# A tuned attention-and-two-MLPs kernel: a fourth raw weight buffer, two q/k buffers, a shorter warm-up, and a new order

## The chip, the cores and the metric

The kernel runs on one core of a Trainium2 chip. The metric is the device time of one execution in microseconds. The kernel before took 869.03 us (median of three runs, 868.75 to 869.29).

## What is computed

Attention over 4 sequences of 576 tokens with 8 heads of 64, causal within a window of 128 and with a linear distance bias; then two MLPs on the 2304 x 512 result, 512 to 2048 and back. The first has a rational activation, the second x * sigmoid(x).

```python
mask = (rel >= 0) & (rel < 128)                     # rel = query - key
attn = softmax(where(mask, q @ k.T / 8 - slope[h] * rel, -1e9))
x = (attn @ v).reshape(2304, 512)
h = x @ w_in;  P = a0 + a1*h + a2*h**2 + a3*h**3
x = (P / (1 + |b0|*|h| + |b1|*h**2 + 1e-6)) @ w_out
h = x @ w2_in;  out = (h / (1 + exp(-h))) @ w2_out
```

The MLP weights arrive as 64-bit floats, so a raw tile of 128 x 512 weights is 512 KB.

## The kernel before

**Arithmetic.** Each MLP operand is split in two rounded parts, high and low (`xh` and `xl`, `gh` and `gl`, two halves of a weight tile), and each product is three matmuls: high x high, high x low, low x high. The second MLP uses a seven-product scheme for 2 x 2 blocks (`CHAIN`), so its weights are first combined into seven "forms", which are written to memory (`prep`) and streamed back (`stream_in`).

**Stages.** The 18 token tiles are cut into blocks of 4, 4, 3, 4 and 3 tiles. For a block, attention runs in four groups (a pair of heads each): scores on PE (L698), a predicated copy for the masked part (L704) and the masked maximum (L711) on DVE, the exponential on ACT (L715), the row sums' reciprocal on DVE (L726, L727), the normalisation on POOL (L734), transposes on PE (L754), two mask products (L799 and L803 on DVE, or L785 and L786 on POOL), and the product with v on PE (L831). Its result is cut into `xh` on ACT and `xl` on DVE (L855) or, for some groups of block 0, with a further copy on ACT and the subtraction on POOL (L851; option `xl00` to `xl03`). Then come the block's 16 steps of the first MLP (L889 to L891 for `h`, L958 to L960 for `acc`), among which the attention of a later block is mixed. The second MLP runs in three token groups, each with a phase A (`z_a`) and a phase B (`z_b`).

**First-MLP weights.** For each of 16 steps a raw tile of the first weights (`w1`) and one of the second (`wo1`) is loaded by SP (L549), made into fp32 by two steps on ACT (L561, L564) and one on DVE (L567), and split: high part by ACT or POOL (L474), low part by a subtraction on POOL (L485). That subtraction is the last reader of the raw tile. All raw tiles share the tag `wraw` with three buffers (`stb`).

**Order.** No engine chooses its work while the kernel runs: `Plan` is a list scheduler that, while the program is built, places each operation on an engine with assumed costs, assumed DMA landing times (`LAG` is added to what depends on a load) and a priority (lower first; about one unit per step of the first MLP). The order in which it places the operations is the order of each engine's instructions, and an engine waits for the head of its queue. The numbers in `OPT` are engine choices and offsets of priorities: `pw` and `pwo` for the first MLP's weights, `qlead` and `vlead` for the loads of q/k and v, `pw2` and `pwo2` for the forms of the second MLP, `tlead`, `hlead`, `xlead`, `slead` for the second MLP. `SHIFTS` adds a number to the priorities of runs of operations.

**Spins.** `first_spin` issues `warm` matmuls on the identity, whose result nobody reads. While the program is emitted, gaps of over 300 planned ns on PE in the first part are filled with more:

```python
if free is not None and o.start - free > OPT["fillmin"] and not first_acc and not (first_h and live):
    pl.spin(int((o.start - free) * OPT["fill"] / c_pe4(P)), ...)     # c_pe4(128) = 215.8, fill = 0.6
```

The planner's times for the start are: identity ready on POOL at 700 + 600, 89 to PE, `warm` x 427, 110 for a stall; the first q/k load issued at 730, landed at 730 + 2000 + 720, then `LAG` 1400 and 100.

**q and k.** Each group loads `kd` and `qd` (L627; L636 for the first group, in two parts) into a ring of `qkb` buffers each.

Of the kernel before, what the change touches and what calls it, by code (L numbers as in the profile page):

```python
# [9 lines left out]
F32 = mybir.dt.float32  # L10
F32R = mybir.dt.float32r
I32 = mybir.dt.int32
# [8 lines left out]
NT, DM, DFF = B * S, H * D, 2048  # L21
P = 128
# [10 lines left out]
OPT = {  # L33
    'blk1': '4,4,3,4,3',
    'res': 0,
    'lag': 2,
    'gh': 'act|pool',
    'gl': 'dve|pool',
    'whi': 'act|pool',
    'wlo': 'pool',  # L40
    'norm': 'pool',
# [4 lines left out]
    'hb': 2,  # L46
    'eb': 2,
    'ptb': 1,
    'qkb': 3,
    'vb': 3,  # L50
    'tabs': 'pool',
    'stb': 3,
    'strb': 3,
    'wpro': 0.256,
    'dS': -1.52,
    'dT': 0.037,
    'dA': 0.149,
    'dm': 0.366,
    'look': 0.451,
    'pw': -0.72,  # L60
    'pwo': -0.374,
    'dg': -5.616,
    'lead': 2.536,
    'slk': 0,
    'warm': 6,
    'fill': 0.6,
    'fillmin': 300.0,
    'fs': 10,
    'ob': 3,
    'pl': -0.721,  # L70
    'vlead': -1.233,
    'qlead': -1.974,
    'keen': 9999.0,
    'norm0': 'pool',
    'sq': 'act',
# [4 lines left out]
    'mk02': 'dd',  # L80
    'mk03': 'dd',
    'xl00': 'd',
    'xl01': 'd',
    'xl02': 'p',
    'xl03': 'd',
    'alt': 0,
    'gh0': 'act|dve',
    'gl0': 'pool',
    'la': 8.921,
    'lb': 302.617,  # L90
    'dm2': 1.231,
    'sums': 'pool',
    'fhi': 'act|pool',
    'flo': 'dve|pool',
# [1 line left out]
    'xsum': 'dve|pool',  # L96
    'xfh': 'act|pool',
    'xfl': 'pool',
    's1': 'act',
    'tsum': 'pool',  # L100
    'th': 'act|dve',
    'tl': 'dve|pool',
    'tlead': 1.016,
    'hlead': -0.505,
    'oq': 'sp',
    'pw2': 511.696,
    'rw2': 25.851,
    'pwo2': 1331.915,
    'rwo2': 14.569,
    'xlead': -0.854,  # L110
    'slead': 0.691,
    'shift': 'act',
    'tail': 1,
}
# [1 line left out]


SHIFTS = [
# [6 lines left out]
]  # L125


# [28 lines left out]
           for b in ("pe", "act", "dve", "pool", "sp")}  # L156
LATENCY["pe", "pe"] = 0
PORT_GAP = 60.0
LAG = {"kd": 1400.0, "qd": 1400.0, "vh": 1400.0, "wraw": 1200.0, "ws": 400.0, "wv": 400.0, "tab": 0.0}
FREE0 = (700.0, 730.0)  # L160
STALL = 110.0

# [9 lines left out]
class Plan:  # L172
# [11 lines left out]
    def op(self, prio, eng, cost, fn, reads=(), writes=(), after=(), dma=False):  # L184

        o = Op()
        o.eng, o.cost, o.fn, o.prio, o.idx = eng, cost, fn, prio, len(self.ops)
        o.alts = eng if isinstance(eng, dict) else {eng: (cost, fn)}

        o.banks = {t[:2] for t in list(reads) + list(writes) if t[0] in ("h", "atA", "atB") or t[0].startswith("acc")}  # L190
        o.port = {e for e in o.alts if e == "pool" or e == "dve" and not o.banks}
        o.deps, o.allocs = set(after), []
        o.dma = dma or eng == "sp"
        o.lag = max([LAG.get(t[0], 0.0) for t in writes], default=0.0) if o.dma else 0.0
        for t in list(reads) + list(writes):
            key, reg = t[:2], t[2:]
            if key not in self.tile_ops:
                self.tile_ops[key] = []
                o.allocs.append(key)
            else:  # L200
                o.deps.add(self.tile_ops[key][0])
            self.tile_ops[key].append(o)
        for t in reads:
            key, reg = t[:2], t[2:]
            for w, r in self.writers.get(key, ()):
                if not reg or not r or r == reg:
                    o.deps.add(w)
        for t in writes:
            key, reg = t[:2], t[2:]
            for w, r in self.writers.get(key, ()):  # L210
                if not reg or not r or r == reg:
                    o.deps.add(w)
            for w, r in self.readers.get(key, ()):
                if not reg or not r or r == reg:
                    o.deps.add(w)
        for t in reads:
            self.readers.setdefault(t[:2], []).append((o, t[2:]))
        for t in writes:
            self.writers.setdefault(t[:2], []).append((o, t[2:]))
        o.deps.discard(o)  # L220
        self.ops.append(o)
        return o
# [166 lines left out]
def plan_kernel(ctx, tc, qn, kn, vp, table, w1, wo1, w2, wo2, out):  # L389
    nc = tc.nc if tc is not None else None  # L390
    BLK1 = [int(x) for x in OPT["blk1"].split(",")]
    NMAX = max(BLK1) * P
    NB1MAX = max(BLK1)
    RES, LAG = OPT["res"], OPT["lag"]
    pl = Plan()
# [12 lines left out]
    act = pool("act", OPT["actb"])  # L408
    gpool = pool("g", OPT["gb"])
    evac = pool("evac", OPT["ob"])  # L410
    stage = pool("stage", OPT["stb"])
# [9 lines left out]
    def apool(name, bufs):  # L421
        return att_stack.enter_context(tc.tile_pool(name=name, bufs=bufs)) if tc is not None else None
# [4 lines left out]
    pt_p = apool("pt", OPT["ptb"])  # L427
    st_p = apool("st", 4)
    tab_p = apool("tabs", 1)
    for t in ("kd", "qd"):  # L430
        pl.tag(t, OPT["qkb"])
    pl.tag("vh", OPT["vb"])
# [81 lines left out]
        T[("h", "spin")] = h_p.tile([P, 512], F32, tag="h", name="spin")  # L514
        spin(OPT["warm"])

    pl.op(-98, "pe", 427 * OPT["warm"], first_spin, reads=[("ident", 0)], writes=[("h", "spin")])
    pl.spin = spin

    late = []  # L520

    def late_consts():
        for part, cols in ((0, slice(0, 3 * P)), (1, slice(3 * P, 6 * P + 16))):
            pl.op(-91.0 + 0.5 * part, "sp", 700, lambda cols=cols: nc.sync.dma_start(tab_all[:, cols], table[:, cols]), writes=[("tab", part)])
        for part in range(2):
            for h in range(H):
                pl.op(-70 + 0.1 * h + 10 * (h // 2) + 25 * part, do_copy("act" if h + part == 0 else OPT["tabs"], 2 * P,
                      lambda h=h, part=part: (tabs[:, h, 2 * part:2 * part + 2], tab[:, 4 * part:4 * part + 2]), scale=-8.0 * 2.0 ** -(h + 1)), 0, None,
                      reads=[("tab", part)], writes=[("tabs", h, part)])
        late.append(("na", 0))  # L530
        late.append(("ab", 0))
        pl.op(-3, "dve", 80, lambda: nc.vector.tensor_scalar(out=na, in0=coef[:, 0:4], scalar1=-1.0, scalar2=None, op0=ALU.mult),
              reads=[("tab", 1)], writes=[("na", 0)])
        pl.op(-3, "act", 200, lambda: nc.scalar.activation(out=ab, in_=coef[:, 4:6], func=AF.Abs), reads=[("tab", 1)], writes=[("ab", 0)])
# [6 lines left out]
        return r[:, :, 1].bitcast(F32) if wide else r  # L541

    def raw_weight(name, f, src, p, load_p):
        rk = ("wraw", f"{name}{f}")

        def load():
            if wide:
                raw = stage.tile([P, DM, 2], I32, tag="wraw", name=f"raw_{name}{f}")
                nc.sync.dma_start(raw, src.bitcast(I32).rearrange("p (c two) -> p c two", two=2))  # L549
            else:  # L550
                raw = stage.tile([P, DM], F32, tag="wraw", name=f"raw_{name}{f}")
                nc.sync.dma_start(raw, src)
            T[rk] = raw

        pl.op(load_p, "sp", 1500 if wide else 728, load, writes=[rk])
        if wide:


            top = lambda: T[rk][:, :, 1].bitcast(F32)
            low = lambda: T[rk][:, :, 0].bitcast(U32)  # L560
            pl.op(p - 0.6, "act", c_act(NR) + 45, lambda: nc.scalar.activation(out=top(), in_=top(), func=AF.Prelu, scale=2.0 ** -112, alpha=2.0 ** 32),  # L561
                  reads=[rk + (1,)], writes=[rk + (1,)])
            pl.op(p - 0.5, any_of(OPT["shift"], {
                "act": (c_act(NR) + 45, lambda: nc.scalar.activation(out=low(), in_=low(), func=AF.Copy, scale=LOW_SCALE)),  # L564
                "dve": (c_dve2x(NR), lambda: nc.vector.tensor_scalar(
                    out=low(), in0=low(), scalar1=29, scalar2=None, op0=ALU.logical_shift_right))}), 0, None, reads=[rk + (0,)], writes=[rk + (0,)])
            pl.op(p - 0.3, "dve", c_dve(NR), lambda: nc.vector.scalar_tensor_tensor(  # L567
                out=top().bitcast(U32), in0=top().bitcast(U32), scalar=3, in1=low(), op0=ALU.logical_shift_left, op1=ALU.bitwise_or),
                reads=[rk], writes=[rk + (1,)])
        return rk  # L570
# [421 lines left out]
    lead = OPT["lead"]  # L992
# [65 lines left out]
        pools["v"] = ctx.enter_context(tc.tile_pool(name="stream2", bufs=3))  # L1058
        pools["s"] = ctx.enter_context(tc.tile_pool(name="xsums", bufs=2))

    last_att = [o for k, l in pl.tile_ops.items() if k[0] in ("kd", "qd", "vh", "e", "ph", "m", "l", "tab", "tabs") for o in l]
    opener = pl.op((nb1 - 1) * KF + 1.0, "sp", 0, open2, after=last_att)
    for j in range(NF):
        pl.tag(f"F{j}", 1)
# [395 lines left out]
```

## Time and profile before

| | |
|---|---|
| Median of three runs | 869.03 us |
| Profiled execution | 869.16 us |
| Its span | 867.3 us |
| PE / DVE / ACT / POOL busy | 855.2 / 643.1 / 603.1 / 637.9 us |
| Moved by DMA | 228.94 MB, 264 GB/s on average |

Times in the trace are microseconds from the start of the span. PE is TensorE, DVE VectorE, ACT ScalarE, POOL GpSimd, SP the engine that issues most loads. Matmuls overlap, so the time from one start to the next says more than a matmul's own duration. A wait is named by what it waited for last.

### The profile page before, as it was taken

How to read it: one execution, taken by the hardware profiler on the slowest of the kernel's cores; microseconds unless marked ns; L12 is line 12 of the kernel's file. 1: busy time of each engine (PE TensorE's matmuls, PEld its weight loads, DVE VectorE, ACT ScalarE, POOL GpSimd, SP SyncE). 2: the span in 40 equal slices, each digit the busy share in tenths (PEclk: the TensorE clock that was granted, in tenths of full speed). 3: DMA queues.
4: the chain of work that ended last, by engine and by line, in shares of the span. 5: the costliest groups of instructions: out<-in, count | busy, mean ns of one | idle time of the engine just before them, and what ended most of it. 6: DMA issues, size and time to landing. Idle time of an engine off the chain costs nothing.

```text
span 867.3 us, 15300 instructions
## 1 busy us (share of the span) xinstructions
PE 855.2 (99%) x5076; PEld 765.1 (88%) x5076; DVE 643.1 (74%) x1308; ACT 603.1 (70%) x1291; POOL 637.9 (74%) x613
## 2 busy tenths in 40 slices
PE   8989999999999999999999999999999999999998
PEld 6667778877788998777889999999999999999998
DVE  7899897789999898998889984357733477433652
ACT  6699997799888988887889984446434365344452
POOL 4778845666888897878899677479954599744884
PEclk9999999999999999999999999999999999999999
DMA  7746764586889887876797889898888888878884
GB/s 253 264 161 214 243 223 137 169 277 227 289 310 321 294 280 263 306 255 238 275 349 240 295 297 356 262 318 281 281 277 250 292 288 282 295 248 258 252 269 169
DMA packets 80462, 228.94 MB, mean 264 GB/s; under 512 B 8192, under 2 KB 17152, under 8 KB 80384
## 3 DMA queue, kind: packets, MB, share of 16 engines
q1 hardware_dynamic: 78080, 219.59, 76.2%
q10 hardware_dynamic: 2304, 8.39, 2.4%
q8 instruction: 40, 0.66, 0.3%
q14 instruction: 38, 0.31, 0.1%
HBM read 178.66 MB, written 49.28 MB: 263 GB/s over the span
## 4 chain that ended last, share of the span: by engine, by line
PE 82%; DVE 5%; ACT 4%; POOL 3%; DMA 3%; issue 2%; SPq 0%; ACTq 0%; POOLq 0%; DVEq 0%
PE acc L958 6%; PE h L889 6%; PE acc L960 6%; PE acc L959 6%; PE h L891 5%; PE h L890 5%; PE z_a L1233 4%; PE z_b L1300 4%; PE z_a L1234 4%; PE z_a L1235 4%; PE z_b L1301 4%; PE z_b L1299 4%; PE bank_atA L831 3%; PE bank_atA L698 2%; PE bank_atA L1233 1%
## 5 line engine op out<-in xcount | busy, mean ns | idle before, releaser
L485 POOL TENSOR_TENSOR xl_b<-g,xh_b 128x384 fp32r<-128x384 f32 x81 | 90.6, 1119 | 69.6 <-ACT xh_b L466 67.8
L466 ACT CAST xh_b<-g 128x384 fp32r<-128x384 f32 x162 | 83.0, 514 | 64.3 <-PE z_b L1301 42.0
L958 PE MATMUL acc<-gh,wo 128*128 128x512 f32 (+1 forms) x320 | 121.1, 378 | 0.0
L960 PE MATMUL acc<-gl,wo 128*128 128x512 f32 (+1 forms) x320 | 118.7, 371 | 0.1
L959 PE MATMUL acc<-gh,wo 128*128 128x512 f32 (+1 forms) x320 | 117.8, 368 | 0.0
L481 DVE TENSOR_TENSOR xl_b<-g,xh_b 128x384 fp32r<-128x384 f32 x87 | 87.3, 1014 | 30.3 <-ACT xh_b L466 29.1
L485 POOL TENSOR_TENSOR gl<-t,gh 128x512 fp32r<-128x512 f32 (+1 forms) x76 | 93.0, 1224 | 15.9 <-ACT gh L466 12.5
L385 ACT ACTIVATE g<-t_a 128x384 f32<-128x384 f32 x72 | 37.9, 526 | 75.2 <-DVE t_a L378 75.2
L485 POOL TENSOR_TENSOR g<-g,g 128x384 f32<-128x384 f32 x72 | 84.5, 1185 | 2.0
L889 PE MATMUL h<-xh,ws 128*128 128x512 f32 (+1 forms) x224 | 84.2, 376 | 0.4 <-DVE t L934 0.4
L891 PE MATMUL h<-xh,ws 128*128 128x512 f32 (+1 forms) x224 | 82.2, 367 | 0.0
L890 PE MATMUL h<-xl,ws 128*128 128x512 f32 (+1 forms) x224 | 82.1, 367 | 0.0
L958 PEld LDWEIGHTS acc<-gh,wo 128*128 128x128 f32 x320 | 60.1, 188 | 13.4 <-issue 5.6
L960 PEld LDWEIGHTS acc<-gl,wo 128*128 128x128 f32 x320 | 60.0, 188 | 9.5 <-POOL gl L485 1.5
L959 PEld LDWEIGHTS acc<-gh,wo 128*128 128x128 f32 x320 | 60.1, 188 | 6.7
L1233 PE MATMUL z_a<-xf,w2s 128*128 128x384 f32 x192 | 64.2, 335 | 0.0
L1235 PE MATMUL z_a<-xf,w2s 128*128 128x384 f32 x192 | 64.1, 334 | 0.0
L1234 PE MATMUL z_a<-xf,w2s 128*128 128x384 f32 x192 | 64.1, 334 | 0.0
L1299 PE MATMUL z_b<-xh_b,wo2s 128*128 128x384 f32 x192 | 64.1, 334 | 0.0
L1300 PE MATMUL z_b<-xl_b,wo2s 128*128 128x384 f32 x192 | 64.1, 334 | 0.0
L1301 PE MATMUL z_b<-xh_b,wo2s 128*128 128x384 f32 x192 | 64.1, 334 | 0.0
L715 ACT ACTIVATE e<-e,m 128x128 f32<-128x128 f32 x144 | 56.0, 392 | 7.6 <-DVE m L711 7.3
(207 smaller groups left out, 2701.9 us busy)
## 6 DMA issues: line engine op xcount, KB each, us to landing
w2s<-forms_w SPq DMA_DIRECT2D x84, 512.0 KB, 4.7
wo2s<-forms_wo SPq DMA_DIRECT2D x84, 512.0 KB, 4.6
ws<-sc SPq DMA_DIRECT2D x64, 512.0 KB, 4.4
raw_w<-in_w SPq DMA_DIRECT2D x32, 512.0 KB, 4.9
raw_wo<-in_wo SPq DMA_DIRECT2D x32, 512.0 KB, 4.9
forms_w<-st_w SPq DMA_DIRECT2D x24, 512.0 KB, 5.0
forms_wo<-st_wo SPq DMA_DIRECT2D x24, 512.0 KB, 4.9
sc<-w ACTq DMA_DIRECT2D x16, 512.0 KB, 5.2
```

Of the source, the lines that this page charges most:

```text
L485: nc.gpsimd.tensor_tensor(out=o, in0=a, in1=b, op=op)
L889: nc.tensor.matmul(o, lhsT=T[W][:, 0, c], rhs=xh, start=kt == 0, stop=False)
L890: nc.tensor.matmul(o, lhsT=T[W][:, 0, c], rhs=xl, start=False, stop=False)
L891: nc.tensor.matmul(o, lhsT=T[W][:, 1, c], rhs=xh, start=False, stop=kt == KD - 1)
L958: nc.tensor.matmul(a, lhsT=T[WO][:, 0, c], rhs=T[G1][:, :n], start=first_f, stop=False)
L959: nc.tensor.matmul(a, lhsT=T[WO][:, 1, c], rhs=T[G1][:, :n], start=False, stop=False)
L960: nc.tensor.matmul(a, lhsT=T[WO][:, 0, c], rhs=T[G2][:, :n], start=False, stop=last_f)
L1233: nc.tensor.matmul(o, lhsT=w(0, kt * P), rhs=x[:, 0, kt], start=st and kt == 0, stop=False, skip_group_check=True)
L1234: nc.tensor.matmul(o, lhsT=w(0, kt * P), rhs=x[:, 1, kt], start=False, stop=False, skip_group_check=True)
L1235: nc.tensor.matmul(o, lhsT=w(1, kt * P), rhs=x[:, 0, kt], start=False, stop=kt == 1, skip_group_check=True)
L1299: nc.tensor.matmul(o, lhsT=w(0, m * P), rhs=h, start=st and q == 0, stop=False, skip_group_check=True)
L1300: nc.tensor.matmul(o, lhsT=w(0, m * P), rhs=l, start=False, stop=False, skip_group_check=True)
```

## The change

The raw tiles of the first MLP's odd second weights (`wo1`, f = 1, 3, ...) get a tag and a pool of one buffer of their own; this pool closes with the attention's pools. The rings of `kd` and `qd` have two buffers in place of three. `warm` is 3 in place of 6. In the planner the warm-up and the table loads are assumed longer, and `LAG` is not added for a tile with index 0, which is the first group's `kd`, `qd` and `vh`. Four engine choices change (`xl01`, `gl0`, `s1`, `th`), many priority offsets change, and `SHIFTS` is a new list (only its first entries are shown), so the order on every engine is planned anew.

```diff
-    'qkb': 3,
+    'qkb': 2,
-    'wpro': 0.256,
-    'dS': -1.52,
-    'dT': 0.037,
-    'dA': 0.149,
-    'dm': 0.366,
-    'look': 0.451,
-    'pw': -0.72,
-    'pwo': -0.374,
-    'dg': -5.616,
-    'lead': 2.536,
+    'wpro': 0.249,
+    'dS': -1.551,
+    'dT': -0.036,
+    'dA': 0.112,
+    'dm': 0.165,
+    'look': 2.085,
+    'pw': -0.374,
+    'pwo': 0.042,
+    'dg': -2.108,
+    'lead': 2.551,
-    'warm': 6,
+    'warm': 3,
-    'pl': -0.721,
-    'vlead': -1.233,
-    'qlead': -1.974,
+    'pl': 0.045,
+    'vlead': -2.618,
+    'qlead': -0.035,
-    'xl01': 'd',
+    'xl01': 'p',
-    'gl0': 'pool',
-    'la': 8.921,
-    'lb': 302.617,
-    'dm2': 1.231,
+    'gl0': 'dve|pool',
+    'la': 17.853,
+    'lb': 163.905,
+    'dm2': -0.281,
-    's1': 'act',
+    's1': 'act|dve',
-    'th': 'act|dve',
+    'th': 'act',
-    'tlead': 1.016,
-    'hlead': -0.505,
+    'tlead': 21.962,
+    'hlead': -5.152,
-    'pw2': 511.696,
-    'rw2': 25.851,
-    'pwo2': 1331.915,
-    'rwo2': 14.569,
-    'xlead': -0.854,
-    'slead': 0.691,
+    'pw2': 67.228,
+    'rw2': 2.912,
+    'pwo2': 2440.758,
+    'rwo2': 12.704,
+    'xlead': -33.586,
+    'slead': 1.745,
 SHIFTS = [
-    (47, 4, -0.61), (257, 3, 0.14), (291, 1, 1.63), (341, 4, 0.79), (437, 26, -0.03), (546, 6, 0.48), (734, 76, 0.18), (882, 57, -0.68),
+    (73, 1, 2.51), (181, 1, 0.25), (282, 12, 1.4), (332, 11, 0.63), (497, 25, 0.81), (532, 42, 0.22), (565, 62, 0.01), (644, 63, 0.03),
...
-LAG = {"kd": 1400.0, "qd": 1400.0, "vh": 1400.0, "wraw": 1200.0, "ws": 400.0, "wv": 400.0, "tab": 0.0}
+LAG = {"kd": 1400.0, "qd": 1400.0, "vh": 1400.0, "wraw": 1200.0, "wrawA": 1200.0, "ws": 400.0, "wv": 400.0, "tab": 0.0}
-        o.lag = max([LAG.get(t[0], 0.0) for t in writes], default=0.0) if o.dma else 0.0
+        o.lag = max([LAG.get(t[0], 0.0) for t in writes if t[1] != 0], default=0.0) if o.dma else 0.0
+    raw_p = apool("raw", 1)
+    pl.tag("wrawA", 1)
-    pl.op(-98, "pe", 427 * OPT["warm"], first_spin, reads=[("ident", 0)], writes=[("h", "spin")])
+    pl.op(-98, "pe", 470 * OPT["warm"], first_spin, reads=[("ident", 0)], writes=[("h", "spin")])
-            pl.op(-91.0 + 0.5 * part, "sp", 700, lambda cols=cols: nc.sync.dma_start(tab_all[:, cols], table[:, cols]), writes=[("tab", part)])
+            pl.op(-91.0 + 0.5 * part, "sp", 1150, lambda cols=cols: nc.sync.dma_start(tab_all[:, cols], table[:, cols]), writes=[("tab", part)])
-        rk = ("wraw", f"{name}{f}")
+        own_pool = name == "wo1" and f % 2
+        rk = ("wrawA" if own_pool else "wraw", f"{name}{f}")
-                raw = stage.tile([P, DM, 2], I32, tag="wraw", name=f"raw_{name}{f}")
+                raw = (raw_p if own_pool else stage).tile([P, DM, 2], I32, tag=rk[0], name=f"raw_{name}{f}")
-    last_att = [o for k, l in pl.tile_ops.items() if k[0] in ("kd", "qd", "vh", "e", "ph", "m", "l", "tab", "tabs") for o in l]
+    last_att = [o for k, l in pl.tile_ops.items() if k[0] in ("kd", "qd", "vh", "e", "ph", "m", "l", "tab", "tabs", "wrawA") for o in l]
```

## Rows read from the trace of the kernel before

**Rows 1.** The page's first part: busy us, share of the span, instructions of each engine.
```profile
PE 855.2 (99%) x5076; PEld 765.1 (88%) x5076; DVE 643.1 (74%) x1308; ACT 603.1 (70%) x1291; POOL 637.9 (74%) x613
```

**Rows 2.** Windows: stretch, length, busy us per engine (instructions), granted clock, DMA share, GB/s.
```profile
0.00:60.00 60.00, 52.92 (x471) 38.64 (x471) 50.03 (x191) 44.13 (x145) 39.14 (x52) 1.00 0.70 239
515.00:863.00 348.00, 348.00 (x2008) 347.58 (x2007) 181.66 (x250) 159.04 (x316) 243.23 (x207) 1.00 0.85 275
...
700.00:750.00 50.00, 50.00 (x291) 50.00 (x290) 36.42 (x40) 25.05 (x48) 48.31 (x35) 1.00 0.87 279
...
10.00:12.00 2.00, 1.53 (x28) 1.22 (x30) 1.93 (x17) 2.00 (x13) 1.26 (x4) 1.00 1.05 405
```

**Rows 3.** Waits of PE from 60 us on: total us, times, longest.
```profile
PE h L889 <- DVE t L934: 1.6, 2, 1.2
```

**Rows 4.** PE's spins in 0 to 60 us: xcount, busy us, mean ns, idle before.
```profile
L511 PE MATMUL spin<-ident 128*128 128x128 f32 x62 | 10.6, 322 | 1.4 <-POOL ident masks.py:199 1.4
...
L511 PE MATMUL bank_acc<-ident 128*128 128x128 f32 x38 | 5.4, 283 | 0.0
```

**Rows 5.** Timeline of the start: start us, us, engine line op, tiles, xcount [idle before].
```profile
0.74 0.38 SPq L636 DMA_DIRECT2D kd<-in_kn  x1
1.17 0.42 SPq L636 DMA_DIRECT2D qd<-in_qn  x1
1.36 3.78 PE L511 MATMUL spin<-ident 128*128 128x128 f32 x16 [1.36 <-POOL ident masks.py:199]
4.47 0.42 ACT L466 ACTIVATE tabs<-tab 128x256 f32<-128x256 f32 x1 [2.46 <-DMA tab<-in_table]
5.07 0.57 PE L698 MATMUL bank_atA<-kd,qd 64*128 64x128 f32 x1
6.18 1.16 PE L511 MATMUL spin<-ident 128*128 128x128 f32 x8
6.30 0.29 DVE L704 COPY_PREDICATED bank_atA<-tab,bank_atA 128x128 f32<-128x128 uint32 x1 [2.11 <-PE bank_atB L698]
```

**Rows 6.** DMA issues of 0 to 1.6 us, then 4.9 to 5.9 us: KB, median us to landing.
```profile
kd<-in_kn SPq DMA_DIRECT2D x1, 128.0 KB, 2.2
qd<-in_qn SPq DMA_DIRECT2D x1, 128.0 KB, 2.1
...
qd<-in_qn SPq DMA_DIRECT2D x1, 256.0 KB, 5.3
```

**Rows 7.** Timeline of POOL: bias tables of the second part, first normalisation.
```profile
7.06 4.33 POOL L474 TENSOR_SCALAR tabs<-tab 128x256 f32<-128x256 f32 x10 [0.65 <-DMA tab<-in_table]
...
12.00 2.04 POOL L734 TENSOR_TENSOR e<-e,l 128x512 f32<-128x512 f32 x2 [0.61 <-DVE l L727]
```

**Rows 8.** Timeline around the third group's scores: SP, PE and DVE.
```profile
7.00 1.81 SPq L549 DMA_DIRECT2D raw_w<-in_w  x3
10.85 0.34 PE L698 MATMUL bank_atA<-kd,qd 64*128 64x128 f32 x1 [0.47 <-DMA qd<-in_qn]
...
15.31 0.29 DVE L711 CUSTOM_DVE_ANT_0 e<-bank_atA,tabs 128x128 f32<-128x128 f32 x1 [1.18 <-PE bank_acc L754]
15.53 0.69 DVE L799 TENSOR_TENSOR ph<-bank_acc,tab 128x512 f32<-128x512 f32 x1
...
16.94 0.51 DVE L803 TENSOR_TENSOR ph<-bank_acc,ph 128x384 f32<-128x384 f32 x1
```

**Rows 9.** Timeline and chain of 31 to 42 us: subtractions, raw tile, ACT's wait.
```profile
31.35 0.68 DVE L855 TENSOR_TENSOR xl<-bank_acc,xh 128x512 fp32r<-128x512 f32 x1
32.89 1.31 POOL L485 TENSOR_TENSOR w<-raw_w,w 128x512 fp32r<-128x512 f32 x1
34.23 6.79 DMA raw_w<-in_w
38.63 1.28 POOL L851 TENSOR_TENSOR xl<-xf,xh 128x512 fp32r<-128x512 f32 x1
41.09 0.69 ACT L561 ACTIVATE raw_w<-raw_w 128x512 f32<-128x512 f32 x1 [3.35 <-DMA raw_w<-in_w]
```

More of the change, by code (lines that the diff above doesn't have):

```diff
@@ L543, in raw_weight @@
     def raw_weight(name, f, src, p, load_p):
-        rk = ("wraw", f"{name}{f}")
+        own_pool = name == "wo1" and f % 2
+        rk = ("wrawA" if own_pool else "wraw", f"{name}{f}")
         def load():
             if wide:
-                raw = stage.tile([P, DM, 2], I32, tag="wraw", name=f"raw_{name}{f}")
+                raw = (raw_p if own_pool else stage).tile([P, DM, 2], I32, tag=rk[0], name=f"raw_{name}{f}")
                 nc.sync.dma_start(raw, src.bitcast(I32).rearrange("p (c two) -> p c two", two=2))
             else:
-                raw = stage.tile([P, DM], F32, tag="wraw", name=f"raw_{name}{f}")
+                raw = (raw_p if own_pool else stage).tile([P, DM], F32, tag=rk[0], name=f"raw_{name}{f}")
                 nc.sync.dma_start(raw, src)
```

10 rows, old and new, of the table SHIFTS are left out of this document.

## Prediction

> **What bounds the kernel now.** The page comes first: TensorE is busy 99% of the span and no other compute engine above 74% [rows 1]. A busy PE need not be doing useful work, so the windows come next: from 515 to 863 us PE is busy 348.00 of 348 us [rows 2], and the waits from 60 us to the end come to 1.6 us in two waits, the longer 1.2 us [rows 3]. After 60 us an order can therefore give back at most 1.6 us, and can lose without limit. The first 60 us are different: 10.6 + 5.4 = 16.0 us of PE's "busy" time there are spins (L511: matmuls on the identity whose result nobody reads), and PE is idle for another 60 - 52.92 = 7.1 us [rows 2, 4]. Attention of block 0 runs there through PE, DVE (50.03 of 60 us), ACT (44.13) and POOL (39.14) [rows 2]: no engine is full, the chain between them is the bound. So the change is priced in the first 60 us, and what starts earlier there reaches the end only if the 800 us behind it stay as dense.
>
> **Shorter warm-up and the planner's landing time.** The first real matmul starts at 5.07 us, behind 16 spin instructions that last from 1.36 to 5.14 [rows 5]. An fp32 matmul shows as two instructions, so these are 8: six asked for, two fillers. The count comes from the code. Before: the spins end for the planner at 1389 + 6 x 427 + 110 = 4061 ns, the first scores at 3450 + 1400 + 100 = 4950, and int(889 x 0.6 / 215.8) = 2. After: 1389 + 3 x 470 + 110 = 2909; the lag of 1400 no longer counts for group 0, so 3550; int(641 x 0.6 / 215.8) = 1. That is 4 matmuls, 8 instructions, half of 3.78 us: over at about 1.36 + 1.9 = 3.3 us. The data are there by then: k is issued at 0.74 and lands 2.2 us later, q at 1.17 and 2.1 us later, so 2.9 and 3.3 us [rows 5, 6]. First scores at about 3.4 us in place of 5.07: 1.65 us earlier. What is late next? The DVE mask (L704), at 6.30 now, needs 1.15 us of scores and the first table, for which ACT waited until 4.47: 4.6 us, so DVE keeps the 1.65. POOL doesn't: it scales ten of the bias tables from 7.06 on, when the second table has landed, until 7.06 + 4.33 = 11.39 us, and the first normalisation (L734), which stands on the chain, starts at 12.00 [rows 5, 7]. On that branch only 0.61 us can be kept. The ends are 0.6 and 1.65; I take the middle, -1.1, since the chain leaves POOL for DVE and PE again at 14 us.
>
> The warm-up could also be doing something. The spins come in groups of 16 in 3.78 us (0.24 each) at the start and 8 in 1.16 us (0.14) from 6.18 on; the granted-clock column says 1.00 throughout [rows 2], but the spacing says 1.2 GHz at first and 2.4 GHz after some 6.2 us [rows 5]. By the Trainium skill (TensorE: Matmul & The Clock Gate, "What's actually happening") the throttled clock is the default and sustained activity lifts it, a rule that speaks against taking half the spins away. By it the sum would be that of rival 3; by the rows, in which the rise comes when the first scores are done and not at a count of spins, it is the one worked out above. No run here shows a shorter warm-up.
>
> **Two buffers for q and k.** The q/k load of a group now waits for the scores of the group two before. From the fourth group on the loads run behind those scores today or have a whole group's time to land, so I cost them at 0. The third group is the exception. Its q load is issued at 5.43 and lands 5.3 us later, at 10.7; its scores wait 0.47 us for it and start at 10.85 [rows 6, 8]. Now they wait for the last scores of group 0 (8.3 us now, about 7.0 then). SP doesn't stand still: two v tiles and three raw tiles (issued from 7.00 on now) go ahead, by the new `qlead` and `vlead` the v tiles behind q/k but free of a wait. At 405 GB/s [rows 2] 512 KB take 1.3 us and 256 KB 0.65, so q lands at about 10.7 + 2 x 0.65 + 3 x 1.3 = 15.9 us. Who waits? DVE's maximum (L711) of that group, and it starts only at 15.31 anyway, behind the transposes of group 0 which free its `e` buffer; DVE then has two mask products (L799) and two differences (L803) of group 0, 2 x (0.69 + 0.51) = 2.4 us, that can go first [rows 8]. Below: 0; above: 15.9 + 1.2 from first scores to mask (5.07 to 6.30 in group 0) + 2 x 0.29 for two masks - 15.31 = +2.4 [rows 5, 8]. I take 0, by the cover of 2.4 us.
>
> **The fourth raw buffer.** Loads of raw tiles (512 KB) wait in the ring of three until POOL has subtracted (L485). Which load matters? The one issued at 34.23, released by POOL's subtraction from 32.89 to 34.20, takes 6.8 us to land, and ACT stands idle 3.35 us until 41.09 with exponentials of the next group behind it; the chain runs right through it [rows 9]. It is the sixth load: three first weights, one second, two first. The new buffer takes the odd second weights out of the ring, and they come after it. So this load still waits for the third one's subtraction, and the buffer by itself gives 0 there. It frees only later ones, and PE shows no wait for a weight [rows 3]. One indirect gain: `pw` sets the splits 0.35 steps later, so ACT's raw tile may come behind the exponentials it now blocks. Bounds 0 and -3.35; I take a third, -1.0.
>
> **The other edits.** `xl01: p` moves the second group's subtraction from DVE (0.68 us) to POOL (1.28) with a further copy on ACT; both engines are on the chain at times: -0.7 to +1.3, taken 0 [rows 9]. Preparation of w2 from priority 511 to 67: PE's two waits after 60 us are both for DVE's t, none for a form; 0 [rows 3]. The edits in the second MLP (casts on ACT alone, other lead times) have the cover of 348 us without a wait; POOL is the fullest there, 48.31 of 50 us from 700 to 750 [rows 2]. New `SHIFTS` reorder everything within these covers: -1.6 (all PE waits after 60 us gone) to +2, taken 0.
>
> **Sum.** -1.1 - 1.0 = -2.1 us. The profiled execution took 869.16 us (span 867.3, 1.9 outside it), 0.13 above the median of 869.03; 869.03 - 2.1 = 866.9 us, -0.24%.
>
> **Rivals.**
> 1. The early start is absorbed: only POOL's 0.6 us are kept, ACT's block stays, the rest cancels. For it: POOL's tables bound by the second landing, and a ring that is the same for the load at 34.23. Against it: DVE and ACT both wait less from 4.6 us on. 868.4 us: within 0.2% (1.7 us, what a measurement tells from no change).
> 2. Slower, by the third group's q/k. The place is SP between 5 and 8 us. If the first odd second weight, whose buffer is free from the start, is also issued ahead (another 1.3 us), q lands at 17.2 and the maximum starts 2.4 + 1.3 = 3.7 us late; with half of DVE's 2.4 us used and 0.6 kept from the start, +1.9: 870.9 us. It decides from a landing later than about 15.9, where DVE's 2.4 us of other work run out. For it: nothing else holds that raw tile back. Against it: the tile's priority is behind the first three.
> 3. The clock rises later for want of spins. The scores between 7 and 12 us fill about 3 us of PE; the first half group takes 6.30 - 5.07 = 1.2 us at the lower level [rows 5], and at the upper not under half of that, so five of them cost at most 5 x 0.6 = 3.0 us more; with two thirds of it behind DVE's work +1.0 is left, less 0.6 kept: 869.4 us. By the Trainium skill's rule the trace of the changed kernel would show spins 0.2 us apart beyond 6.2 us.
> 4. POOL fills in the second MLP: PE waits there. POOL has 1.7 us left of 50 in the worst window; two further tiles of 1.1 us on it per group, three groups, less the room: about +3 from the point at which POOL has no gap, 869.0 - 1.1 + 3 = 870.9 us. Against it: `tl` may still choose DVE, which is busy 36 of 50 us there.
>
> **Chances.** Forecast 0.47 (own range 864 to 867.3); rival 1 0.29; rival 2 0.11; rival 3 0.05; rival 4 0.08. Faster by over 0.2%: 0.47. Within 0.2%: 0.29 + 0.05 = 0.34. Slower: 0.19. Range: below, -1.65 - 3.35 and a third of the 1.6 us of PE waits: 863.5; above, to rivals 2 and 4: 871.0.
>
> **What would show it.** Right: 8 spin instructions, first scores near 3.4 us, the first normalisation on POOL at 11.4, ACT's wait for a raw tile under 2.5 us, 348 us of the second MLP without a wait, PE waits after 60 us still under 2. Wrong: q/k of the third group landing after 16 us with DVE idle; a wait of over 3 us for a raw tile on ACT again; spins 0.2 us apart after 7 us; PE waits for POOL after 515 us.

## The result and the profile after

The changed kernel takes 875.21 us (median of 4, 873.81 to 877.17) where the kernel before takes 868.89 beside it (median of 4): a ratio of 1.0070, 95% interval 1.0055 to 1.0084. It is slower by 6.3 us, where a gain of 2.1 us was forecast and 871.0 was the upper end of the range. The profiled execution took 875.43 us, 6.27 more than that of before.

First the page of the changed kernel, its busy line and the line of the chain that ended last, by engine.

```profile
PE 858.6 (98%) x5092; PEld 766.5 (88%) x5092; DVE 653.3 (75%) x1311; ACT 606.4 (69%) x1294; POOL 630.1 (72%) x608
...
PE 71%; DVE 12%; ACT 6%; DMA 6%; POOL 3%; issue 3%; SPq 0%; POOLq 0%; DVEq 0%; ACTq 0%
```

PE did 3.4 us more "busy" work than in [rows 1], and POOL 7.8 less. In the chain PE has 71% where the same line of before has 82%; DVE went from 5 to 12% and DMA from 3 to 6%: a larger share of the time to the end now hangs on something other than PE.

Where the time went is easiest to see as a lag: how much later than before PE starts the matmul that has the same amount of matmul work ahead of it (matmuls counted from the trace, each form at its usual spacing). It is -1.2 us at the first scores, about +4 between 14 and 22 us, back to +1.9 at 60 us, about +4 at 300, +5 at 430 and +6.3 from 534 us to the end, flat. The values at 60 us and at the end hold whichever way the forms are weighed, those between are estimates; each comes from one profiled execution. So two losses: +1.9 in the first 60 us, +4.4 between 60 and 534 us, and nothing in the second MLP behind that. The windows of the changed kernel (stretch, length, busy us per engine, granted clock, DMA share, GB/s) show PE's part of it:

```profile
0.00:60.00 60.00, 52.80 (x467) 39.09 (x468) 48.24 (x189) 45.30 (x144) 43.22 (x55) 1.00 0.75 258
60.00:190.00 130.00, 129.43 (x683) 101.61 (x681) 115.97 (x238) 114.41 (x229) 85.73 (x79) 1.00 0.59 195
190.00:403.00 213.00, 211.51 (x1316) 173.08 (x1315) 194.02 (x457) 186.77 (x424) 172.60 (x180) 1.00 0.84 286
403.00:520.00 117.00, 115.47 (x619) 104.00 (x618) 108.19 (x181) 99.82 (x186) 94.28 (x97) 1.00 0.82 273
520.00:870.00 350.00, 349.05 (x2014) 348.70 (x2012) 186.34 (x247) 160.11 (x316) 234.27 (x199) 1.00 0.84 271
```

Those of the kernel before for the three middle stretches:

```profile
60.00:190.00 130.00, 128.82 (x663) 101.91 (x660) 111.48 (x224) 114.98 (x225) 86.61 (x80) 1.00 0.61 200
190.00:403.00 213.00, 212.57 (x1347) 174.08 (x1346) 199.20 (x479) 188.10 (x427) 174.93 (x183) 1.00 0.82 281
403.00:520.00 117.00, 116.85 (x618) 106.73 (x617) 102.52 (x171) 100.60 (x190) 97.91 (x98) 1.00 0.83 287
```

PE's idle time in these three stretches was 1.18 + 0.43 + 0.15 = 1.8 us and is 0.57 + 1.49 + 1.53 = 3.6 us. The waits of PE from 60 us on (total us, times, longest), three largest of seven groups, answer to [rows 3]:

```profile
PE h L892 <- DVE t L937: 1.9, 4, 0.7
PE z_a L1236 <- ACT x L468: 0.9, 1, 0.9
PE acc L961 <- DVE x L982: 0.5, 1, 0.5
```

In place of two waits there are ten: on DVE's last step of the activation (L937, which was L934), on an evacuation by ACT, on a sum by DVE and others. The start, answering to [rows 5, 7, 8] (start us, us, engine line op, tiles, count, idle before):

```profile
1.36 2.08 PE L513 MATMUL spin<-ident 128*128 128x128 f32 x8 [1.36 <-POOL ident masks.py:199]
...
3.86 0.55 PE L701 MATMUL bank_atA<-kd,qd 64*128 64x128 f32 x1 [0.42 <-DMA qd<-in_qn]
...
4.76 0.42 ACT L468 ACTIVATE tabs<-tab 128x256 f32<-128x256 f32 x1 [2.74 <-DMA tab<-in_table]
...
5.44 2.07 PE L513 MATMUL spin<-ident 128*128 128x128 f32 x8
...
7.32 4.33 POOL L476 TENSOR_SCALAR tabs<-tab 128x256 f32<-128x256 f32 x10 [0.62 <-DMA tab<-in_table]
...
9.44 0.74 SPq L630 DMA_DIRECT2D qd<-in_qn  x1
...
10.22 0.45 SPq L552 DMA_DIRECT2D raw_wo<-in_wo  x1
...
12.27 2.04 POOL L737 TENSOR_TENSOR e<-e,l 128x512 f32<-128x512 f32 x2 [0.63 <-DVE l L730]
...
15.26 2.40 PE L513 MATMUL spin<-ident 128*128 128x128 f32 x20
...
16.40 0.69 DVE L802 TENSOR_TENSOR ph<-bank_acc,tab 128x512 f32<-128x512 f32 x1
...
17.59 0.37 PE L701 MATMUL bank_atA<-kd,qd 64*128 64x128 f32 x1
...
20.48 0.27 DVE L707 COPY_PREDICATED bank_atA<-tab,bank_atA 128x128 f32<-128x128 uint32 x1
...
20.89 0.29 DVE L714 CUSTOM_DVE_ANT_0 e<-bank_atA,tabs 128x128 f32<-128x128 f32 x1
```

And the landing of the third group's q, issued at 9.44 us (KB, us to landing), which answers to [rows 6]:

```profile
qd<-in_qn SPq DMA_DIRECT2D x1, 256.0 KB, 7.0
```

Eight spin instructions, as forecast; first scores at 3.86 us (forecast 3.4: they wait 0.42 us for q), the mask's table at 4.76 (forecast 4.6). But the next spins still stand 0.26 us apart (2.07 for 8) where the same eight took 1.16 in [rows 5]; the second tables begin at 7.32 and the first normalisation at 12.27, not at 11.4; q of the third group lands at 16.4 and its scores follow a block of spins at 17.59. No engine waits for that q. DVE is busy with its other work from 16.40 on, and the third group's mask (L707) stands behind that work, at 20.48, its maximum (L714) at 20.89, 5.6 us later than in [rows 8]. One forecast gain is there: ACT's wait of 3.35 us for a raw tile [rows 9] is gone, and its largest wait at a raw tile in the first 60 us is now 0.9 us, for POOL's subtraction.

### The profile page after: what moved, and what is told of

Read it like the earlier page. It is cut to its first block, busy times and chain, and to the rows that moved or that the text cites. A ratio compares the mean times of both kernels' runs of the same rounds, so it can differ in the third digit from the quotient of the medians.

```text
span 873.6 us, 15318 instructions
## 1 busy us (share of the span) xinstructions
PE 858.6 (98%) x5092; PEld 766.5 (88%) x5092; DVE 653.3 (75%) x1311; ACT 606.4 (69%) x1294; POOL 630.1 (72%) x608
## 4 chain that ended last, share of the span: by engine, by line
PE 71%; DVE 12%; ACT 6%; DMA 6%; POOL 3%; issue 3%; SPq 0%; POOLq 0%; DVEq 0%; ACTq 0%
PE h L892 5%; PE h L894 4%; PE h L893 4%; PE acc L961 4%; PE acc L963 4%; PE acc L962 4%; PE z_b L1303 4%; PE z_b L1302 4%; PE z_b L1304 4%; PE z_a L1236 4%; PE z_a L1237 4%; PE z_a L1238 4%; PE bank_atA L701 2%; PE bank_atA L834 2%; DMA forms_wo<-st_wo 1%
## 5 line engine op out<-in xcount | busy, mean ns | idle before, releaser
L468 ACT CAST xh_b<-g 128x384 fp32r<-128x384 f32 x168 | 86.1, 514 | 68.0 <-PE z_b L1304 43.5
L483 DVE TENSOR_TENSOR xl_b<-g,xh_b 128x384 fp32r<-128x384 f32 x86 | 90.7, 1062 | 26.3 <-ACT xh_b L468 25.2
L487 POOL TENSOR_TENSOR gl<-t,gh 128x512 fp32r<-128x512 f32 (+1 forms) x65 | 79.9, 1230 | 18.9 <-ACT gh L468 16.8
```

The lines of the kernel that those rows point to most:

```text
L487: nc.gpsimd.tensor_tensor(out=o, in0=a, in1=b, op=op)
```

## The experiments

Ratios are to the kernel before on the same chip, with 95% intervals. "Lag" is as above, from each kernel's one profiled execution, against that of before. It is uncertain by some 1.5 us, as the two profiles of the changed order below differ by, with its spins as they are and put back; executions of before on one chip lie up to 3.9 us apart.

**Fewer spins alone.** The order of before, with four warm-up matmuls.

```diff
-        spin(OPT["warm"])
+        spin(3)
...
+                    if not hasattr(pl, "filled"):
+                        pl.filled, n_fill = True, 1
```

> The kernel before with its own order on every engine, but 4 warm-up matmuls (8 instructions) ahead of the first scores in place of 8 (16). Theory 'clock' (the spins lift the clock, and half of them lift it late): first scores near 3.8 us, spins still 0.21 us apart until about 9 us, score groups 1.5 us long in place of 1.0, end +0.3 to +1.5 us (869.2 to 870.4). Rival 'head start' (my prediction): the 1.2 us at the first scores are kept in part, end -0.6 to -1.2 us (867.7 to 868.3).

Measured: 1.0002 (0.9990 to 1.0014), no difference: the forecast gain is not there, and the loss of theory 'clock' at most at its lower end. Its PE timeline, then the same half group in the kernel before:

```profile
3.81 0.55 PE L698 MATMUL bank_atA<-kd,qd 64*128 64x128 f32 x1 [0.38 <-DMA qd<-in_qn]
...
5.39 2.07 PE L511 MATMUL spin<-ident 128*128 128x128 f32 x8
7.39 0.58 PE L698 MATMUL bank_atA<-kd,qd 64*64 64x192 f32 x1
```

```profile
7.31 0.54 PE L698 MATMUL bank_atA<-kd,qd 64*64 64x192 f32 x2
```

The head start of 1.26 us is there at 3.81 and gone at 7.39, where the second half of the first group starts in both kernels within 0.1 us: the eight spins in front of it last 2.07 us at the lower clock where they lasted 1.16 [rows 5]. From 11 us on the lag is +0.2 to +0.4. In this execution the lower clock takes back what the shorter warm-up gives. That it is not the only thing that does, the last experiment shows.

**The spins put back into the changed kernel.**

```diff
-        spin(OPT["warm"])
+        spin(6)
...
+                        pl.filled, n_fill = True, 2
```

> The changed kernel with its own order, but 8 warm-up matmuls (6 and 2) ahead of the first scores in place of 4. Theory 'clock': clock up at about 6.2 us in place of 9, first scores at 5.1 in place of 3.9, and the second half of them no later than now: end -0.3 to -1 us against 875.2 (874.2 to 874.9). Rival 'head start': end +0.6 to +1.2 (875.8 to 876.4).

Measured: 1.0064 (1.0049 to 1.0080); the lag is about +4 at 14 and 22 us and +2.0 at 60 us, as without them. The warm-up isn't what made the change slower. Theory 'clock', at its small end (874.90 against 875.21), can't be told from no difference; the rival's loss isn't there.

**Late q and k alone.** Before, but SP issues the third group's k and q behind the three raw tiles; buffers and every engine's order stay.

```diff
+    moved = [load("kd", 2), load("qd", 2)]
...
+    at = pl.seq.index(load("wraw", "w12")) + 1
+    pl.seq[at:at] = moved
```

> The kernel before with its own order, except that SP issues the third group's q and k behind the three first raw tiles, where the changed kernel has them. Theory 'late q/k' (the two buffers for q and k cost the start): third group's scores at about 16 us in place of 10.85, DVE, whose order is fixed here, stands still for it, end +2 to +5 us (871 to 874). Rival 'covered' (my prediction): DVE's other work hides it, end within 0.5 us of 868.9.

Measured: 1.0080 (1.0065 to 1.0095), more than the +2 to +5 us of the theory, and the lag is +6.7 at 45 us and never given back (+7.2 at the end). Its timeline around the third group's scores, then windows of two microseconds (granted clock third from the end):

```profile
15.95 0.55 PE L698 MATMUL bank_atA<-kd,qd 64*128 64x128 f32 x1 [5.10 <-DMA qd<-in_qn]
...
17.64 0.30 DVE L704 COPY_PREDICATED bank_atA<-tab,bank_atA 128x128 f32<-128x128 uint32 x1 [5.33 <-PE bank_atB L698]
```

```profile
11.00:13.00 2.00, 0.00 (x0) 0.00 (x0) 1.28 (x11) 2.00 (x11) 0.93 (x2) 1.00 1.03 420
13.00:15.00 2.00, 0.00 (x0) 0.00 (x0) 0.00 (x0) 0.85 (x3) 1.51 (x2) 0.70 1.02 391
15.00:17.00 2.00, 1.05 (x8) 0.84 (x12) 0.00 (x0) 0.00 (x0) 0.00 (x0) 0.50 0.57 209
17.00:19.00 2.00, 2.00 (x25) 1.19 (x18) 0.57 (x3) 0.00 (x0) 0.00 (x0) 0.50 0.04 8
...
21.00:23.00 2.00, 1.15 (x12) 0.96 (x10) 1.16 (x6) 1.09 (x7) 0.00 (x0) 1.00 0.48 183
```

The scores wait 5.10 us for q, DVE's masks (L704), which stand ahead of all its other work, wait behind them, and DVE is idle with the 2.4 us of products queued behind a mask that can't run. These engines took their instructions in the written order: work that is ready covers a wait only if it is written ahead of it. On top, while PE waits, the granted clock falls to 0.50 (1.2 GHz) and stays there beyond 17 us, so that the late scores also run at half speed; that is how a wait of 5.1 us becomes a lag of 6.7.

**Early q and k in the changed kernel.** Three q/k buffers again (64 bytes a partition are missing, which one buffer of the maxima's and sums' small tiles pays for), the third group's loads right behind the second's, its fillers dropped; the changed order otherwise.

```diff
-    qk_p = apool("qk", OPT["qkb"])
+    qk_p = apool("qk", 3)
...
-    st_p = apool("st", 4)
+    st_p = apool("st", 3)
...
+    at = pl.seq.index(load("qd", 1)) + 1
+    pl.seq[at:at] = moved
```

> The changed kernel with its own order, but three buffers each for q and k (the 64 bytes that this lacks come from a third instead of a fourth buffer for the row sums), the third group's q and k issued right behind the second's, and the ten filler matmuls ahead of the third group's scores left out. Theory 'late q/k': scores of the third group at about 15.5 in place of 17.6 us, lag at 60 us falls from +1.9 to near 0, end -1.5 to -2.5 us against 875.2 (872.7 to 873.7). Rival 'order' (the order planned around the late load keeps the engines where they are): end -0.5 or less.

Measured: 1.0081 (1.0063 to 1.0100), lag +2.6 at 60 us: no gain, so theory 'late q/k' fails. PE and DVE of the third group, then PE's next instruction and the window behind it:

```profile
14.94 0.37 PE L701 MATMUL bank_atA<-kd,qd 64*128 64x128 f32 x1
...
20.05 0.27 DVE L707 COPY_PREDICATED bank_atA<-tab,bank_atA 128x128 f32<-128x128 uint32 x1
...
21.02 0.54 PE L701 MATMUL bank_atA<-kd,qd 64*64 64x192 f32 x2 [3.79 <-DVE m L714]
```

```profile
22.00:24.00 2.00, 2.00 (x21) 0.85 (x15) 1.60 (x10) 1.43 (x7) 2.00 (x2) 0.50 1.01 408
```

With q issued at 4.96 us and landed 5.3 us later, the scores come 2.65 us earlier than in the changed kernel, the mask 0.43: DVE has other work ahead of it in either case. The order was laid out around the late load, and an early landing does not move an instruction forward in it. The run isn't a clean test of the rest, since without the ten fillers PE stands idle for 3.79 us and the clock falls behind that.

**The buffers in the order of before.** Two q/k buffers alone (loads moved behind the scores that free them, two raw tiles behind the third group's; the moves aren't shown); the fourth raw buffer alone (for which the pool of the maxima and sums goes from four to three); and all three parts together.

```diff
-    qk_p = apool("qk", OPT["qkb"])
+    qk_p = apool("qk", 2)
...
```

> The kernel before with its own order, but two real buffers each for q and k: a group's load stands on SP behind the last scores of the group two before, and the third group's stands behind one raw tile instead of three (the other two follow it). Theory 'late q/k': third group's scores at about 13 us in place of 10.85; DVE, whose mask for them stood at 11.88, is held about 2 us; lag of about +2 us at 20 us which nothing gives back; end 870.8 to 872. Rival 'covered': within 0.5 us of before.

```diff
-    st_p = apool("st", 4)
+    st_p = apool("st", 3)
...
+    raw_p = apool("raw", 1)
...
+                own = name == "wo1" and f % 2
+                raw = (raw_p if own else stage).tile([P, DM, 2], I32, tag="wrawA" if own else "wraw", name=f"raw_{name}{f}")
```

> The kernel before with its own order, but a buffer of its own for the odd second raw tiles (a fourth in all), q and k with three. My prediction of this part: PE waits for no weight, so within 0.4 us of before. Rival 'collision': loads that no longer wait come earlier and delay q, k and v of the fifth and sixth groups: +0.5 to +1.5 us. Rival 'relief': SP stands less in front of a raw tile, ACT's wait of 3.35 us at 41 us shrinks by over 1 us: -0.5 to -1.5.

> All three named changes on the old order: two q/k buffers as in b_qk2, the fourth raw buffer, 4 warm-up matmuls. Theory 'order' (what the changed kernel loses after 60 us, 4.4 us of its 6.3, belongs to its new order and not to the buffers): the sum of the parts at 60 us and less than 0.5 us more from there to the end; 870.8 to 872. Rival 'buffers' (the buffers make those later waits): the lag grows by 3 us or more after 60 us; 874 to 876.

Measured: 1.0048 (1.0034 to 1.0062), 0.9999 (0.9990 to 1.0008) and 1.0033 (1.0021 to 1.0044): the first somewhat above the range of its theory, the second as my prediction had it, the third as theory 'order' has it behind 60 us. With two q/k buffers the third group's k and q, issued at 9.16 and 9.53 us, land at 12.8 and 13.5, and DVE's first mask of that group shows the stall, against the line of before:

```profile
14.68 0.30 DVE L704 COPY_PREDICATED bank_atA<-tab,bank_atA 128x128 f32<-128x128 uint32 x1 [2.36 <-PE bank_atB L698]
```

```profile
11.88 0.30 DVE L704 COPY_PREDICATED bank_atA<-tab,bank_atA 128x128 f32<-128x128 uint32 x1
```

The lag is +3.7 at 60 us and +3.0 at the end; with all three parts +4.2 and +3.5. The raw buffer costs and gives nothing that can be measured. In the order of before none of the three parts loses anything behind 60 us.

**New orders.** First the changed structure with the order searched anew; then three q/k buffers with the fourth raw buffer, six warm-up matmuls and an order searched for that. Some engine choices and many priorities differ with it (not shown).

```diff
-    'look': 2.085,
+    'look': 0.988,
...
 SHIFTS = [
-    (73, 1, 2.51), (181, 1, 0.25), (282, 12, 1.4), (332, 11, 0.63),
...
+    (247, 8, -0.11), (291, 1, 1.63), (341, 4, 0.79), (546, 6, 0.48),
...
```

> The structure of the changed kernel (two q/k buffers, the fourth raw buffer, three warm-up matmuls) with another order of the instructions, searched anew for just this structure. Theory, the written order made the later loss: after 60 us nearly all of the 4.4 us goes (1 us or less is left), and the prologue's 2 to 4 us stay, since q and k of the third group still come late; total 871 to 873. Rival, the buffers themselves make the later waits: the loss after 60 us stays at 3 us or more, total 874 or above.

> The fourth raw buffer with three q/k buffers (one buffer fewer in the pool of store tiles makes the room), six warm-up matmuls instead of eight, and an order searched anew for it. Theory, the two q/k buffers were what cost the prologue and the order of the changed kernel what cost the rest: no lag at 60 us beyond 0.5 us, total 868 to 869. Rival, a new order loses some microseconds on the chip whatever it was searched for, since the durations it was planned with are not the chip's: 870 or above.

Measured: 1.0078 (1.0062 to 1.0094) and 1.0088 (1.0071 to 1.0105). Both theories failed, and the figures of both rivals came. In the prologue the kernels behave as the theories have it: lag at 60 us +2.3 with two q/k buffers, 0.0 with three. But behind 60 us they lose 5.8 and 7.5 us, more than the changed kernel, with two q/k buffers and with three. About half of the 7.5 comes at one place, DVE and POOL first, then PE:

```profile
306.81 3.57 DVE L724 TENSOR_SCALAR l<-l 128x8 f32<-128x8 f32 x1
...
309.32 1.03 POOL L482 TENSOR_TENSOR gl<-t,gh 128x384 fp32r<-128x384 f32 x1
...
316.30 0.44 PE L887 MATMUL h<-xh,ws 128*128 128x384 f32 x1 [2.23 <-DVE t L932]
```

L724 adds a constant to eight columns of row sums; the median of its 20 executions is 0.17 us. This one is written where POOL has four instructions in a row, from 306.34 to 310.35, and it ends as the last of them ends. DVE is 3.4 us late by it, PE waits 2.23 us, and the granted clock falls behind the wait (0.50 from 318 to 320 us). That DVE was held by POOL is read from these times alone; no run isolates it.

**Another order, everything else as before.** Only the planner's nudges differ, chosen so that the plan is as long as that of before and its first 60 us are the same. Two draws:

```diff
 SHIFTS = [
-    (47, 4, -0.61), (257, 3, 0.14), (291, 1, 1.63), (341, 4, 0.79),
...
+    (257, 3, 0.14), (291, 1, 1.63), (341, 4, 0.79), (437, 26, -0.03),
...
```

> The kernel before with its buffers, its warm-up and its first 60 us untouched; only the planner's nudges (SHIFTS) are others, so that 872 of the 4149 instructions behind 60 us stand behind another one on their engine, in an order that the kernel's own plan holds to be as long as the one of before. Theory, the order by itself costs time on the chip, whatever the buffers: the plan's durations and landing times aren't the chip's, and another order loses what this one does not; no lag at 60 us, then 2 to 5 us by the time the second MLP begins; total 871 to 874. Rival, orders that the plan holds equal run equal, and the changed kernel's later loss came from waits that its plan shows too: 868.6 to 869.9.

> The same with another draw of nudges: 845 of the 4149 instructions stand behind another one, the first 60 us as before, the plan's length as before. Theory (the order by itself): again 871 to 874, with its stalls at other places than in the first draw. Rival (equal plans run equal): 868.6 to 869.9.

Measured: 1.0031 (1.0020 to 1.0042) and 1.0004 (0.9996 to 1.0013). The first confirms the theory at its lower end, the second doesn't: 0 to 3 us by the draw. The first loses 3.2 of its 3.6 us behind 60 us at one place (517 to 533 us), where second weights are prepared beside the second MLP's first matmuls. ACT and PE there, then the two transfers that its chain runs through:

```profile
519.60 0.62 ACT L461 CAST st_wo<-sums_wo 128x512 fp32r<-128x512 f32 x1 [1.28 <-DMA forms_wo<-st_wo]
...
529.09 0.62 ACT L461 CAST st_wo<-sums_wo 128x512 fp32r<-128x512 f32 x1 [1.78 <-DMA forms_wo<-st_wo]
...
531.83 0.46 ACT L461 COPY t_a<-z_a 128x384 f32<-128x384 f32 x1
...
532.34 0.44 PE L1228 MATMUL z_a<-xf,w2s 128*128 128x384 f32 x1 [0.90 <-ACT t_a L461]
```

```profile
511.34 9.51 DMA forms_wo<-st_wo
...
523.46 5.56 DMA forms_wo<-st_wo
```

ACT's copy into a store buffer stands idle 1.28 and 1.78 us until an earlier store (9.51 and 5.56 us under way) has freed it; ACT's z_a work is written behind it, and PE waits 0.90 us at 532 behind that. The changed kernel has much the same wait at the same time, with an evacuation buffer:

```profile
530.44 0.48 ACT L468 COPY x<-acc 128x384 f32<-128x384 f32 x1 [2.53 <-DMA x2d<-x]
...
530.97 0.44 PE L1236 MATMUL z_a<-xf,w2s 128*128 128x384 f32 x1 [0.95 <-ACT x L468]
```

and, at 276 us, a sum of DVE's for which DVE stands idle 0.55 us and PE 0.5 us (the third of PE's waits above), until a partial result is back from memory:

```profile
269.14 7.57 DMA x<-part
...
276.73 0.69 DVE x L982
```

**Six warm-up matmuls,** with the order of before and the fourth raw buffer.

```diff
-        spin(OPT["warm"])
+        spin(5)
...
```

> The order of the kernel before, with the fourth raw buffer and six warm-up matmuls instead of eight. Theory, the clock's level decides what an earlier start is worth: the six keep TensorE active until the first scores at about 4.1 us, the step up to the higher clock comes by about 7 us as before, and 0.3 to 1 us of the head start is kept: 868.0 to 868.8. Rival, the start is bound by what comes behind the first scores (tables, masks, the third group's loads): no difference, 868.9 to 869.3.

Measured: 0.9994 (0.9984 to 1.0005): no difference that can be told, so the rival stands. In the profiled execution the spacing says that the higher clock is there at 4.6 us, and the head start of 0.85 us is kept until 8 us; then PE waits for q of the second group, whose scores start at 8.54 in before:

```profile
9.33 0.98 PE L700 MATMUL bank_acc<-kd,qd 64*128 64x128 f32 x12 [1.58 <-DMA qd<-in_qn]
```

So an early clock alone does not carry the head start through. No version here is faster than the kernel before by more than the noise.

## Why the prediction was wrong

By its own steps:

- **Two buffers for q and k: "I take 0, by the cover of 2.4 us". This step failed.** The landing was right (15.9 forecast, 16.4 measured). But whether ready work covers a wait depends on the written order. Where the masks stay ahead of that work the wait costs 3.0 to 3.7 us for a landing at 13.5 and 7.2 for one at 15.8 (two q/k buffers and late q alone, both in the order of before). The changed order does put the cover ahead, and then the mask is late by the cover: DVE works from 16.40 to 20.48 on 2.4 us of products and differences, two steps of raw weights and the row sums, which the step had left out, while the third group's scores, begun at 17.59, wait. With q six us earlier (early q and k) the mask still stands at 20.05. So the +1.9 at 60 us is not a wait for q. It goes with orders that are planned around a late q: the other order searched for two buffers has +2.3, the one searched for three 0.0. I had drawn "below: 0" from DVE's free work and taken that end.
- **The head start: "I take the middle, -1.1". Failed.** By itself it is worth 0 (1.0002). Both reasons against it had been named: POOL's tables are bound by the second table's landing (rival 1), and the clock rises later (rival 3, with 8.8 us in that profile). A third had not: a later group's q can be the next thing to wait for (1.58 us with six warm-up matmuls). No run parts the three. The reading that the clock rises when the first scores are done is not borne out either: with the same 16 spin instructions it rose between 4.8 and 7.6 us (last section).
- **`SHIFTS` and the planner's values: "-1.6 ... to +2, taken 0". The largest miss: +4.4.** I priced it from PE's 1.6 us of waits [rows 3], as if an order that had left so little to wait for were any order's due. What the runs show: the loss behind 60 us goes with the order and not with the buffers. The changed order has it with two q/k buffers, with eight spins and with three q/k buffers (+4.4, +5.9, +5.1; the second from the longest of its six executions, 2.1 us above their median); the order of before has none of it with two q/k buffers, with the raw buffer, with all three parts (-0.7, -0.7, -0.7); two more searched orders have it (+5.8, +7.5), and of two that differ from before only in nudges one has +3.6, the other -0.2.
- **The raw buffer: 0 by itself, right; its indirect gain, -1.0 from ACT's wait: the wait went as forecast [rows 9],** with the changed order and not with the buffer (with the raw buffer alone it is still 2.7 us), but it doesn't show as time against the two losses, and no run isolates it.
- **The second MLP: 0, right from 534 us on** (no PE wait behind that; rival 4 falls). Rival 4's +3 does not follow from its own terms: 2.2 us less the 1.7 of room, three times, is 1.5.

So +1.9 up to 60 us and +4.4 behind it make the +6.3 of the two profiles, and the head start and ACT's shorter wait are not seen in it. Rival 2 had the right sign and named the third group's q and k. But its point, an odd raw tile issued ahead of q, didn't happen (raw_wo goes at 10.22, behind q), DVE was not idle for q as it had it, and it had none of the later loss.

What stays open is what in an order makes the later loss. Part of it is seen: PE's idle time in the middle windows grew by 1.8 us and its wait at 530 us is 0.95 more, 2.8 of 4.4; the rest shows as no idle time of PE, and stays unexplained. In the changed kernel and in the first of the two draws, the long waits that were followed back ended at a transfer whose buffer or result an engine needed ahead of work for PE; in the order searched for three q/k buffers the longest ended at a DVE instruction beside POOL. That these are the causes was not isolated.

## What to carry to other kernels

"Covered by other work on that engine" is only true if that work is written ahead of the waiting instruction; look at the order of the queue, not at the list of what is ready. When a diff replaces a hand-searched order along with a buffer count, price the order as an edit of its own: here 4.4 of the 6.3 us came with it alone, and of two orders equal on paper to the one they replace one took 2.7 us longer (ratio 1.0031) and one no longer. And an early start counts only as far as what comes next lets it through: before counting it, look at the spacing of the matmuls behind it, which tells the clock level, and at the next load that they need.

## What the runs showed of the hardware

In six of the profiles here the granted clock fell behind a wait of PE of 1.6 to 5.1 us. In the run with late q, PE did nothing from 10.9 to 15.95 us; the column stands at 1.00 until 13 us and at 0.50 from 14, and it is back at 1.00 in the window from 21 us. By the Trainium skill (TensorE: Matmul & The Clock Gate, "What's actually happening") the throttled clock is the default and activity releases it; these rows agree, and show its price on a stall: the scores behind the wait stood twice as far apart. The profiled execution of the kernel with six warm-up matmuls (871.33 us, the longest of its 12) shows the same behind a shorter wait: PE is idle for 1.58 us until 9.33, and the level falls some two microseconds later, with PE busy again:

```profile
11.00:12.00 1.00, 0.83 (x8) 0.46 (x6) 0.97 (x10) 0.86 (x5) 0.23 (x1) 0.74 1.06 410
...
13.00:14.00 1.00, 1.00 (x16) 0.49 (x8) 0.45 (x2) 0.19 (x1) 1.00 (x2) 0.50 1.03 418
```

A wait alone doesn't settle it: in the changed kernel PE waits as long, 1.58 us for DVE until 21.45, and the column stays at 1.00. Nor is the wait all that is lost: with two q/k buffers PE waits 2.77 us for q, the column reads 0.60 and 0.54 from 14 to 18 us, and the lag is 3.5 us at 20.

The column doesn't tell of the start, though: it says 1.00 for the first 4 us of every kernel here, while spins 0.24 to 0.26 us apart say 1.2 GHz. When the spacing narrows varies between executions of the same start: with 16 spin instructions ahead of the first scores at 4.8 us in one of the two draws and at 7.1 in the other, at 5.5 in the profile of before and at 7.6 with two q/k buffers; with 12 at 4.6 and 7.2 in two kernels; with 8 between 7.4 and 9.9 in five. So one profile does not price a warm-up; the medians do, and here they show no difference.
